# Chunk 7 transposed ahead of the first block's stores, and two products of a seven-product block exchanged

## The chip, the cores and the metric

The kernel runs on one core of one Trainium2 chip. The metric is the device time in microseconds (us) of one execution. Inside the core several engines work side by side, each through its own list of instructions in order: PE (TensorE, matrix products), DVE (VectorE), ACT (ScalarE), POOL (GpSimd) and SP (SyncE, which here issues nearly all DMAs). They wait for each other through semaphores.

## What is computed

The reference, cut to what matters, is a linear attention with a decaying state, followed by a two-layer network with a Mish-like activation:

```python
# q, k, v: (4, 8, 768, 64); w_in: (512, 2048); w_out: (2048, 512)
for t in range(S):
    state = gamma[None, :, None, None] * state + np.einsum('bhd,bhe->bhde', k[:, :, t], v[:, :, t])
    y[:, :, t] = scale * np.einsum('bhd,bhde->bhe', q[:, :, t], state)
...
x = y.transpose(0, 2, 1, 3).reshape(B * S, H * D)          # 3072 tokens x 512
h = x @ w_in
sp = np.where(h > 20.0, h, np.log1p(np.exp(np.minimum(h, 20.0))))
g = h * np.tanh(sp)
out = (g @ w_out).astype(np.float32)
```

## The kernel before

**Tiles and stages.** The 3072 tokens are 24 chunks of 128 (six for each of the 4 batches). The chunks go through the kernel in blocks: block 0 has four chunks (0 to 3), blocks 1 to 10 have two each, so block 1 has chunks 4 and 5, block 2 has 6 and 7, block 3 has 8 and 9, and so on (`first[blk]` is a block's first chunk).

The attention of a chunk g takes these steps. `load` (L135) brings its q, k and v from memory on SP, 256 KB each. `cast_q` (L320, POOL), `cast_k` (L325, ACT) and `cast_v` (L329, POOL) scale them into fp16. `turn_by_dma` (L342) transposes q and k with one DMA on SP; `turn_and_load` (L902) does that and then issues the loads up to chunk g+2. `scores` (L373) multiplies k and q on PE, `mask` (L383) masks them on DVE, `outer` (L390) makes the outer products of k and v on PE, `state_sum` and `state_decay` carry the state on, and `y_two` (L465) makes the attention's output of a whole block from the state (`past`, L416) and the masked scores (`present`, L423). An ACT copy (L475) then leaves it in `xt`, the input of the network.

The network of a block is `g1` (x times w_in, then Mish) and `g2` (times w_out). From block 1 on, half of the first layer is done by `g1_seven` (L597) in a seven-product scheme for 2 x 2 block matrices: sums of weight blocks (`wsums`) and of input blocks (`tsums`, made by `x_sums`, L588) are multiplied, and the results are combined. From block 2 on the second layer uses a seven-product scheme too (`seven`, L689). Block 1 has the plain second layer (L512).

**Order of the work.** The order on each engine is written out by hand: the program's order is each engine's order. Work of the attention for later chunks is put into named places of a block's network by dictionaries, `steps_of` (L927) for blocks from 2 on and `steps_of_half` (L953) for block 1; a function `step(name)` runs what is listed under a name. Numbered places of block 1's second layer are filled by `plan_of` (L963), among them `scores_two` for chunks 6 and 7 at place 10 and `cast_k` of chunk 10 at place 15, the last one.

**Three accumulators.** `g1_seven` uses three accumulators in PSUM, `pb`, `px` and `pe`. The lines between L653 and L668 are what the change touches. The first product goes to px, and ACT copies it out (`snap`, L623) as m1; px is then not cleared, but added to by the second-sum product `mm(px, s(2), t(2))`, and copied again as u2; later the third-sum product `mm(px, s(3), t(3))` is added to it once more. The first-sum product `mm(pe, s(1), t(1))` starts pe afresh, and its copy is m5. A product that adds to an accumulator can start only when the copy taken from it before is finished. At the place "p2", ahead of these, blocks 2 to 9 have `outer_next`, the outer products of the next block's chunks: eight matmuls for two chunks, or four where the second chunk is the last of its batch, whose state is not needed.

**The queue around the stores.** Block 0 leaves four output tiles of 256 KB in a list `stores`, each with the due number 1; `store_due(n)` (L178) issues on SP all that are due by n. In block 1 that happens at the place "p6". The same place scales chunk 7's k and then has chunk 7 transposed, followed by the loads of chunk 9. `op`, the pool of output tiles, has five of these tiles.

Of the kernel before, what the change touches and what calls it, by code (L numbers as in the profile page):

```python
# [16 lines left out]
def kernel(  # L17
# [21 lines left out]
    BLOCKS = [4] + [2] * ((NCK - 4) // 2)  # L39
    first = [sum(BLOCKS[:i]) for i in range(len(BLOCKS))]  # L40
# [56 lines left out]
    for c in range(2):  # L97
        t = tri_first[c * HB:(c + 1) * HB]
# [79 lines left out]
    def store_due(now):  # L178
        while stores and stores[0][0] <= now:
            _, dst, osb = stores.pop(0)  # L180
            nc.sync.dma_start(dst, osb)
# [251 lines left out]
    def last_of_batch(g):  # L433
        return g % NCH == NCH - 1
# [45 lines left out]
    def win(s, f, bp):  # L480
        return wins[s, f // 2][:, bp, f % 2 * P:(f % 2 + 1) * P]
# [13 lines left out]
    def xt(blk, bp):  # L495
        return xts[0][:, :, bp] if blk == 0 else xts[blk][:, bp, :BLOCKS[blk] * C]
# [13 lines left out]
    def g2_mm(o_ps, blk, t, fb, cols=slice(None)):  # L510
        s, f = divmod(fb, FPS)
        nc.tensor.matmul(  # L512
            o_ps, gts[blk, fb][:, t * P:(t + 1) * P], wouts[s][:, f, cols],
            start=(fb == 0), stop=(fb == NFB - 1))

    def g2_out(o_ps, blk, t, due, cols=slice(None), on_act=False):
        osb = op.tile(list(o_ps.shape), FP32, name="osb", tag="osb")
        if on_act:
            nc.scalar.copy(osb, o_ps)
        else:  # L520
            nc.vector.tensor_copy(osb, o_ps)
        row0 = (first[blk] + t) * P
        dst = out[row0:row0 + P, cols]
        stores.append((due, dst, osb))
# [59 lines left out]
    def x_part(blk, i, j):  # L584
        n = NBP // 2
        return xts[blk][:, i * n:(i + 1) * n, j * P:(j + 1) * P]
# [7 lines left out]
        nc.vector.tensor_tensor(t[:, 2], b[1][1], b[0][1], op=sub)  # L594
        nc.vector.tensor_tensor(t[:, 3], b[1][0], t[:, 1], op=sub)

    def g1_seven(blk, steps):  # L597
        n = NBP // 2
        gt = gtiles[blk, 0] = gp.tile([P, NFB, 2 * P], FP16, name="g", tag="g")
        for fb in range(NFB):  # L600
            gts[blk, fb] = gt[:, fb]
        pb, px, pe = [mmps.tile([P, FPS, P], FP32, name="h_ps", tag="mm") for _ in range(3)]

        def a(i, j):
            return lambda f, d: win(2 * i, f, j * n + d)

        def s(i):
            return lambda f, d: wsums[0][:, i - 1, d, f * P:(f + 1) * P]

        def b(i, j):  # L610
            return lambda d: x_part(blk, i, j)[:, d]

        def t(i):
            return lambda d: tsums[blk][:, i - 1, d]

        def mm(h_ps, w, x, first=False):
            for f in range(FPS):
                for d in range(n):
                    nc.tensor.matmul(  # L619
                        h_ps[:, f], w(f, d), x(d), start=first and f == 0 and d == 0,  # L620
                        stop=d == n - 1, skip_group_check=True)

        def snap(h_ps):  # L623
            x = hsnaps[0][:, nsnap[0] % 4].rearrange("p (f t) -> p f t", t=P)
            nsnap[0] += 1
            nc.scalar.copy(x, h_ps)  # L626
            return x

        def mish_of(i, j, h):
            nc.scalar.activation(  # L630
                gt[:, 2 * i * FPS:(2 * i + 1) * FPS, j * P:(j + 1) * P], h, AF.Mish,
                scale=inv_boost3)

        def plus(h_ps, x):
            h = hp.tile([P, FPS, P], FP32, name="hsum", tag="hsum", bufs=3)
            nc.vector.tensor_tensor(h, h_ps, x, op=ALU.add)  # L636
            return h

        def plain(s, half):
            h_ps = mmps.tile([P, 2, 2 * P], FP32, name="h_ps", tag="mm")  # L640
            for j in range(2):
                for bp in range(NBP):
                    nc.tensor.matmul(  # L643
                        h_ps[:, j], win(s, 2 * half + j, bp), xt(blk, bp),
                        start=bp == 0, stop=bp == NBP - 1)
            fb = s * FPS + 2 * half
            nc.scalar.activation(gt[:, fb:fb + 2], h_ps, AF.Mish, scale=inv_boost3)  # L647

        def step(name):
            for fn, *args in steps.get(name, ()):  # L650
                fn(*args)

        mm(px, a(0, 0), b(0, 0), True)  # L653
        m1 = snap(px)
        mm(pb, a(0, 1), b(1, 0), True)
        c11 = plus(pb, m1)
        step("p2")
        mm(pe, s(1), t(1), True)
        m5 = snap(pe)
        mm(px, s(2), t(2))  # L660
        u2 = snap(px)
        mish_of(0, 0, c11)
        step("p6")
        plain(1, 0)
        mm(px, s(3), t(3))
        c22 = plus(px, m5)
        mm(pe, s(4), b(1, 1))
        c12 = plus(pe, u2)  # L668
        mish_of(1, 1, c22)
        mish_of(0, 1, c12)  # L670
        step("p7")
        plain(3, 0)
        mm(px, a(1, 1), t(4))
        mish_of(1, 0, px)
        step("p4")
        plain(1, 1)
        step("h2")
        plain(3, 1)
        step("end")
# [247 lines left out]
    def steps_of(blk):  # L927
        a, nb = first[blk] + 4, blk + 1
        if nb == len(BLOCKS):
            only, then = lambda *work: [], lambda *work: []  # L930
        else:
            only = lambda *work: list(work)
            then = only if a < NCK else lambda *work: []
        return {
            "p2": [*then((gate_x, blk), (cast_q, a)), *only((outer_next, nb), (sum_next, nb, 0),
                   (decay_next, nb, 0)), (cast_v, a)],
            "p6": [(store_due, 1), (turn_and_load, a)],
            "p7": [(store_due, 2), *only((sum_next, nb, 1)), (sums_a, blk, slice(0, FPS))],
            "p4": [(store_due, 3), (sums_a, blk, slice(FPS, FPS + 2))],
            "h2": only((scores, a - 2), (scores, a - 1), (mask, a - 2)),  # L940
            "end": [(sums_a, blk, slice(FPS + 2, 2 * FPS))],
            "m1": [(cast_k, a + 1)],
            "m2": [*only((gate_g, blk), (decay_next, nb, 1)), (cast_q, a + 1), (cast_v, a + 1),
                   *only((mask, a - 1)), (turn_and_load, a + 1)],
            "m7": [*only((y_two, nb)), (cast_k, a + 2)],
            "m3": only((x_sums, nb)),
        }

    def some_late(n):
        for _ in range(min(n, len(late))):  # L950
            late.pop(0)()

    def steps_of_half(blk):  # L953
        a = first[blk] + 4
        return {
            "p2": [(gate_x, blk), (cast_v, a - 1)],
            "p6": [(store_due, 1), (cast_k, a - 1), (turn_and_load, a - 1), (some_late, 1)],
            "p7": [(store_due, 3), (cast_q, a), (some_late, 1)],
            "p4": [(cast_v, a), (some_late, 2)],
            "end": [(cast_k, a), (turn_and_load, a)],  # L960
        }

    def plan_of(blk):  # L963
        a = first[blk] + 4
        return {10: [(scores_two, blk + 1)],
                11: [(cast_q, a + 1), (cast_k, a + 1)],
                12: [(outer_two, blk + 1), (cast_v, a + 1), (turn_and_load, a + 1)],
                14: [(y_two, blk + 1)],
                15: [(cast_k, a + 2)]}
# [5 lines left out]
    for blk in range(1, len(BLOCKS)):  # L975
        if blk >= SEVEN:
            steps = steps_of(blk)
            g1_seven(blk, steps)
            seven(blk, steps, blk + 1 == len(BLOCKS))
            continue  # L980
        g1_seven(blk, steps_of_half(blk))
        n1 = NFB * BLOCKS[blk] // CPB
        plan = plan_of(blk)
        for u in range(n1, 2 * n1):
            store_due(u)
            t, part = divmod(u - n1, 4)
            if part == 0:
                o_ps = mmps.tile([P, d_model], FP32, name="o_ps", tag="mm")
            for fb in range(part * 4, part * 4 + 4):
                g2_mm(o_ps, blk, t, fb)  # L990
            if part == 3:
                g2_out(o_ps, blk, t, u + 3 if t == 0 else 3)
            for fn, *args in plan.get(u, ()):
                fn(*args)
            some_late(1)
        x_sums(blk + 1)
# [31 lines left out]
```

## Time and profile before

| | |
|---|---|
| median of 3 runs | 204.19 us (203.92 to 204.65) |
| the profiled execution's own time | 204.32 us |
| its span, first to last instruction | 202.4 us |
| PE busy | 194.2 us, 96% |
| PE weight loads busy | 152.9 us, 76% |
| DVE busy | 143.5 us, 71% |
| ACT busy | 111.1 us, 55% |
| POOL busy | 67.8 us, 33% |
| bytes moved by DMA | 38.65 MB |
| granted TensorE clock | full speed all along |

All times below are counted from the span's start. A timeline row gives the start, the duration, the engine, the source line, the operation, what it writes from what it reads, and in square brackets the idle time of the engine before it with what ended that. SPq rows are DMA issues: their duration is that of issuing, and the data lands some microseconds later. Ends of matmuls are modelled and overlap the next ones, so the spacing of starts is what a matmul costs. The chain of waits goes back from the last instruction, at each step to what released it.

### The profile page before, as it was taken

What the parts mean: (1) busy time and instruction counts of PE and PEld (TensorE: products, weight loads), DVE (VectorE), ACT (ScalarE), POOL (GpSimd) and SP (SyncE); (2) the same over time, 40 slices, a digit from 0 to 9 for tenths busy, and PEclk for the clock granted to TensorE, in tenths of its full rate; (3) what the DMA queues carried; (4) which work ended last, traced back from release to release, by engine and by line L of the source; (5) the groups of instructions that cost most, each with busy time, mean ns of one, the idle gap of its engine ahead of it and who ended that gap; (6) DMA issues with size and microseconds to landing.
All of it is one profiled execution on the core that took longest, in us unless ns stands there. A gap on an engine that the chain in (4) does not pass through costs nothing.

```text
span 202.4 us, 5431 instructions
## 1 busy us (share of the span) xinstructions
PE 194.2 (96%) x2239; PEld 152.9 (76%) x2239; DVE 143.5 (71%) x271; ACT 111.1 (55%) x199; POOL 67.8 (33%) x83
## 2 busy tenths in 40 slices
PE   6797999999999999999999999999999999999993
PEld 2455544455955788988988988988988988988982
DVE  2677744969879687587696696787696696696552
ACT  2364665242961773774674674674674663753850
POOL 4073000527424337424407607604407616200000
PEclk9999999999999999999999999999999999999999
DMA  4999999998999998996991992999992952200202
GB/s 164 304 312 359 385 386 292 276 263 182 224 272 230 233 221 177 195 224 161 230 206 38 216 243 81 233 183 156 247 205 46 224 98 55 104 3 25 84 26 78
DMA packets 95896, 38.65 MB, mean 191 GB/s; under 512 B 82304, under 2 KB 89984, under 8 KB 95872
## 3 DMA queue, kind: packets, MB, share of 16 engines
q1 hardware_dynamic: 92608, 37.50, 81.2%
q10 hardware_dynamic: 3264, 0.82, 2.2%
q8 instruction: 17, 0.28, 0.6%
q14 instruction: 7, 0.06, 0.1%
HBM read 27.30 MB, written 6.29 MB: 166 GB/s over the span
## 4 chain that ended last, share of the span: by engine, by line
PE 78%; DMA 14%; ACT 2%; DVE 2%; issue 1%; SPq 1%; POOL 1%; POOLq 0%; DVEq 0%
PE o_ps L709 28%; PE h_ps L643 16%; PE h_ps L619 14%; DMA vf<-in_v_dram 6%; PE h_ps L490 6%; DMA qkt<-qk 3%; PE y_ps L429 3%; DMA qfirst<-in_q_dram 2%; DMA kf<-in_k_dram 2%; PE at L379 2%; PE o_ps L512 2%; PE y_ps L419 2%; PE u_ps L393 2%; PE h_ps L782 1%; SPq L132 1%
## 5 line engine op out<-in xcount | busy, mean ns | idle before, releaser
L643 PE MATMUL h_ps<-xt,win 128*128 128x256 f16 x320 | 41.2, 273 | 0.0
L322 POOL TENSOR_TENSOR qk<-qf,qvs 128x512 f16<-128x512 f32 x20 | 23.7, 1186 | 26.4 <-DMA qf<-in_q_dram 25.5
L643 PEld LDWEIGHTS <-win 128*128 128x128 f16 x320 | 29.4, 98 | 3.6
L709 PEld LDWEIGHTS <-gsum 128*128 128x128 f16 x288 | 27.5, 98 | 3.8
L636 DVE TENSOR_TENSOR hsum<-h_ps,hsnap 128x512 f32<-128x512 f32 x30 | 19.8, 688 | 13.9 <-PE h_ps L619 11.5
L647 ACT ACTIVATE g<-h_ps 128x512 f16<-128x512 f32 x40 | 23.7, 593 | 5.6 <-PE h_ps L643 5.5
L385 DVE TENSOR_TENSOR am<-at,tri 128x1024 f16<-128x1024 f32 x20 | 24.2, 1217 | 1.7 <-PE at L379 1.7
L709 PE MATMUL o_ps<-tmat,gsum 128*128 128x256 f16 x216 | 25.1, 273 | 0.0
L626 ACT COPY hsnap<-h_ps 128x512 f32<-128x512 f32 x30 | 16.6, 587 | 13.2 <-PE h_ps L619 13.2
L331 POOL TENSOR_TENSOR v<-vf,qvs 128x512 f16<-128x512 f32 x20 | 21.3, 1064 | 7.4 <-DMA vf<-in_v_dram 7.4
L709 PEld LDWEIGHTS <-g 128*128 128x128 f16 x216 | 21.1, 98 | 2.4
L723 DVE TENSOR_TENSOR osb<-o_ps,snap 128x256 f32<-128x256 f32 x27 | 11.4, 424 | 16.0 <-PE o_ps L709 11.7
L512 PE MATMUL o_ps<-wout,g 128*128 128x512 f16 x96 | 22.7, 379 | 0.0
L630 ACT ACTIVATE g<-hsum 128x512 f16<-128x512 f32 x30 | 18.7, 634 | 4.3 <-DVE hsum L636 4.3
L619 PEld LDWEIGHTS <-wsum 128*128 128x128 f16 x320 | 19.1, 98 | 0.8
L327 ACT ACTIVATE qk<-kf 128x512 f16<-128x512 f32 x20 | 12.6, 632 | 12.1 <-DMA kf<-in_k_dram 7.4
L475 ACT CAST xt<-y_ps 128x1024 f16<-128x1024 f32 x10 | 10.1, 1012 | 16.2 <-PE y_ps L429 16.2
L715 ACT COPY snap<-o_ps 128x256 f32<-128x256 f32 x27 | 10.1, 372 | 15.7 <-PE o_ps L709 15.7
L709 PE MATMUL o_ps<-wout,g 128*128 128x256 f16 x144 | 17.2, 273 | 0.0
L619 PE MATMUL h_ps<-xsum,wsum 128*128 128x128 f16 x240 | 16.6, 219 | 0.0
L340 POOL COPY gate<-gsum 128x1 f16<-128x1 f16 x8 | 1.5, 186 | 44.2 <-DVE gsum L683 44.2
L619 PEld LDWEIGHTS <-win 128*128 128x128 f16 x240 | 15.1, 98 | 1.5 <-issue 0.8
(96 smaller groups left out, 289.9 us busy)
## 6 DMA issues: line engine op xcount, KB each, us to landing
kf<-in_k_dram SPq DMA_DIRECT2D x23, 256.0 KB, 4.5
vf<-in_v_dram SPq DMA_DIRECT2D x23, 256.0 KB, 5.3
out_dram<-osb SPq DMA_DIRECT2D x22, 256.0 KB, 4.3
qf<-in_q_dram SPq DMA_DIRECT2D x19, 256.0 KB, 4.0
wt<-in_moe_w_out_dram SPq DMA_DIRECT2D x3, 1024.0 KB, 8.1
wi<-in_moe_w_in_dram SPq DMA_DIRECT2D x4, 512.0 KB, 7.1
wi<-in_moe_w_in_dram SPq DMA_DIRECT2D x2, 1024.0 KB, 10.7
qfirst<-in_q_dram SPq DMA_DIRECT2D x2, 512.0 KB, 5.5
```

The costliest lines, as they stand in the source:

```text
L322: nc.gpsimd.tensor_tensor(room16(g)[0], loaded[g][0], qs.unsqueeze(2).broadcast_to((P, H, D)), op=ALU.mult)
L327: nc.scalar.mul(room16(g)[1], loaded[g][1], BOOST)
L331: nc.gpsimd.tensor_tensor(room16(g)[2], loaded[g][2], vs.unsqueeze(2).broadcast_to((P, H, D)), op=ALU.mult)
L385: nc.vector.tensor_tensor(am, ats.pop(g), tri.unsqueeze(1).unsqueeze(1).broadcast_to((P, 2, HP, C)), op=ALU.mult)
L512: nc.tensor.matmul(o_ps, gts[blk, fb][:, t * P:(t + 1) * P], wouts[s][:, f, cols], start=(fb == 0), stop=(fb == NFB - 1))
L619: nc.tensor.matmul(h_ps[:, f], w(f, d), x(d), start=first and f == 0 and d == 0, stop=d == n - 1, skip_group_check=True)
L626: nc.scalar.copy(x, h_ps)
L630: nc.scalar.activation(gt[:, 2 * i * FPS:(2 * i + 1) * FPS, j * P:(j + 1) * P], h, AF.Mish, scale=inv_boost3)
L636: nc.vector.tensor_tensor(h, h_ps, x, op=ALU.add)
L643: nc.tensor.matmul(h_ps[:, j], win(s, 2 * half + j, bp), xt(blk, bp), start=bp == 0, stop=bp == NBP - 1)
L647: nc.scalar.activation(gt[:, fb:fb + 2], h_ps, AF.Mish, scale=inv_boost3)
L709: nc.tensor.matmul(o_ps, x(f), w(f), start=first and f == 0, stop=f == n - 1, skip_group_check=True)
```

## The change

There are two edits. In block 1, `cast_k(7)` moves from the place "p6" to a new place "u2", which is right behind the copy of px as u2 and ahead of the first Mish of the block on ACT. At "p6", `turn_and_load(7)` comes first and the stores follow; the due number there rises from 1 to 3, and the separate `store_due(3)` at "p7" goes. On SP this puts one transposition and the three loads of chunk 9 ahead of the four stores. On ACT it exchanges two neighbours, the scaling and the Mish.

In `g1_seven`, a flag `sum_first` puts the second-sum product and its copy ahead of the first-sum product and its copy. The flag is set where the next block exists and its second chunk is not the last of a batch, that is in blocks 2, 4, 5, 7 and 8. These are the blocks with two chunks' outer products at "p2". No instruction is added or removed on any engine.

```diff
-    def g1_seven(blk, steps):
+    def g1_seven(blk, steps, sum_first=False):
...
         step("p2")
+        if sum_first:
+            mm(px, s(2), t(2))
+            u2 = snap(px)
         mm(pe, s(1), t(1), True)
         m5 = snap(pe)
-        mm(px, s(2), t(2))
-        u2 = snap(px)
+        if not sum_first:
+            mm(px, s(2), t(2))
+            u2 = snap(px)
+        step("u2")
         mish_of(0, 0, c11)
         step("p6")
...
             "p2": [(gate_x, blk), (cast_v, a - 1)],
-            "p6": [(store_due, 1), (cast_k, a - 1), (turn_and_load, a - 1), (some_late, 1)],
-            "p7": [(store_due, 3), (cast_q, a), (some_late, 1)],
+            "u2": [(cast_k, a - 1)],
+            "p6": [(turn_and_load, a - 1), (store_due, 3), (some_late, 1)],
+            "p7": [(cast_q, a), (some_late, 1)],
...
-            g1_seven(blk, steps)
+            g1_seven(blk, steps, blk + 1 < len(BLOCKS) and not last_of_batch(first[blk + 1] + 1))
```

In block 1, `a` is 8, so `a - 1` is chunk 7.

## The prediction

> **What bounds the kernel now.** I read the busy table first (PE, TensorE, is busy 96% of the 202.4 us span), then the chain of waits, which from 61 us to the end is a string of PE pieces. A change can therefore pay only where PE itself stands, and I looked for those places. In the chain and the waits there is one near the edit:
>
> ```profile
> 51.61 3.74 DMA vf<-in_v_dram
> 55.35 5.61 DMA qkt<-qk
> 60.96 0.05 issue
> 61.01 0.40 PE at L379 x8
> ```
> ```profile
> PE at L379 <- DMA qkt<-qk: 0.4, 1, 0.4
> ```
>
> The transposition of chunk 7, issued at 55.35, lands 5.61 us later, and the scores of chunk 7 (L379) wait for it. The timeline (start, duration, engine, line) shows what stood ahead of it on the DMA queue SP, the scaling of its k behind a Mish on ACT (ScalarE), and what undisturbed scores cost:
>
> ```profile
> 52.59 2.60 SPq L181 DMA_DIRECT2D out_dram<-osb  x4
> 55.35 2.46 SPq L344 DMA_TRANSPOSE qkt<-qk  x1
> ```
> ```profile
> 53.36 0.64 ACT L630 ACTIVATE g<-hsum 128x512 f16<-128x512 f32 x1
> 53.89 0.63 ACT L327 ACTIVATE qk<-kf 128x512 f16<-128x512 f32 x1
> ```
> ```profile
> 60.16 0.40 PE L379 MATMUL at<-qkt 64*128 64x128 f16 x8
> 61.01 0.40 PE L379 MATMUL at<-qkt 64*128 64x128 f16 x8 [0.45 <-DMA qkt<-qk]
> 61.34 1.90 PE L512 MATMUL o_ps<-wout,g 128*128 128x512 f16 x8
> ...
> 73.65 0.62 PE L379 MATMUL at<-qkt 64*128 64x128 f16 x16
> 74.20 1.05 PE L643 MATMUL h_ps<-xt,win 128*128 128x256 f16 x8
> ```
>
> Sixteen score products take 74.20-73.65 = 0.55 us in block 2, but 61.34-60.16 = 1.18 here: the stall costs 0.63 us. Six microseconds later, at the start of block 2, comes the piece that decides my forecast:
>
> ```profile
> 67.89 0.63 ACT L327 ACTIVATE qk<-kf 128x512 f16<-128x512 f32 x1 [0.63 <-DMA kf<-in_k_dram]
> 68.42 0.57 ACT L626 COPY hsnap<-h_ps 128x512 f32<-128x512 f32 x1
> ```
> ```profile
> 68.20 0.61 PE L393 MATMUL u_ps<-v,qk 128*128 128x128 f16 x8
> 68.64 1.06 PE L619 MATMUL h_ps<-xsum,wsum 128*128 128x128 f16 x16
> 69.54 1.04 PE L643 MATMUL h_ps<-xt,win 128*128 128x256 f16 x8
> ```
>
> ACT works in the order of the program. Its copy m1 (L626) stands behind the scaling of chunk 10's k (L327), and that waits for the load, which lands at 67.86 (issued 63.68, 4.2 us to landing). So m1 ends at 68.99, 1.13 us behind the landing. PE does not notice today: after the outer products (L393) it runs the first-sum product into pe for 0.45 us (half of 69.54-68.64) and needs m1 only for the second-sum one into px, at 69.09.
>
> **The change part by part.**
>
> (1) *The scores' stall.* cast_k(7) takes the place of the Mish at 53.36 and ends at 53.99 instead of 54.52. SP is free at 52.49 (its last load issue), stands until then, and issues the transposition at about 54.05. With the transposition of chunk 6, issued on an almost equally filled queue, issue to landing took 4.1 us, so chunk 7's lands at 58.2. The scores need it at 60.16 plus half of 0.55, 60.4: 2.2 us of cover. The 0.63 us goes. Behind it nothing takes it back: VectorE's two masks end at 62.95 in both kernels, the copy L521 (62.88 to 63.57) and the state L402 (0.69) behind them end by 64.3, and PE's past product (L419), now at 65.25, would come at 64.62. So block 2 begins 0.63 earlier, at 66.68.
>
> (2) *The Mish moved back* by 0.53 us ends at 54.5; its first reader, the second layer of block 1 (L512), starts at 57.48: 3 us of cover. The work behind it on ACT keeps its place, since both instructions stay ahead of it. It costs nothing; without cover it would cost 0.53.
>
> (3) *The DMA queue.* The transposition and three loads (q, k, v of chunk 9) pass four stores of 256 KB on SP; the next transposition and chunk 10's loads follow the stores. No bytes change, so the landing L of chunk 10's k moves only by idle time made or saved. Spacing of landings now, from issue starts and times to landing: v(8) 56.1; stores to 59.8 (3.7); transposition 61.0 (1.1); q, k, v of chunk 9 62.2, 63.4, 64.5 (1.2 each, 1.1 the last); transposition of 8 65.3 (0.8); q(10) 66.65 (1.35); k(10) 67.86 (1.2). In the stores' 3.7 lies a hole:
>
> ```profile
> 56.00:58.40 2.40, 2.40 (x21) 1.77 (x19) 2.37 (x4) 2.37 (x6) 1.33 (x1) 1.00 1.07 376
> 58.40:59.60 1.20, 1.20 (x7) 0.53 (x6) 0.98 (x2) 0.39 (x1) 0.00 (x0) 1.00 1.31 52
> ```
> ```profile
> q8 instruction: 1, 0.02, 4.8%
> ```
>
> (columns: window, its length, busy time of PE, PEld, DVE, ACT and POOL, clock, DMA share, GB/s). For 1.2 us the engines hold packets but move 52 GB/s instead of 376. The last line is the DMA view of 55.9 to 57.2: one instruction packet of 16 KB held one of the 16 engines for 1 us (4.8% of 16 times 1.3). That engine's share of the stores runs late, and the transposition begins on all engines only when it is through. So the stores really need 2.5 us.
>
> After: transposition issue 54.05 to 55.9 (1.85, as chunk 6's), q(9) issued then and landing 3.5 us later, as the load behind chunk 6's transposition did (50.36 to 53.89): 59.4. Then k 1.2, v 1.1, stores 2.5, transposition 1.0 (after a store elsewhere 0.9 to 1.0), q 1.35, k 1.2: L = 59.4+8.35 = 67.8. Bounds: with the shortest issue (1.24) and q's shortest latency (3.4) q(9) lands at 58.7 and L is 67.05; with the longest issue (2.46) and 4.0 us for q, as behind the transposition of 143.7, q(9) comes at 60.5 and L at 68.8; a transposition kept by the held engine lies inside that. I take 67.8, the row of chunk 6.
>
> The Trainium skill says otherwise of the hole: "DMA: Bandwidth & Descriptors", section "Two DMAs through the same engine are not ordered", states that "Nothing at all orders DMAs across the 16 engines". The window at 58.4 does not agree for a transposition; what that rule gives is a rival below.
>
> (4) *The second-sum product first* (blocks 2, 4, 5, 7, 8). In every block PE stands 0.06 us before the third-sum product: in block 2 it starts at 70.47, eight products of 0.109 behind 69.54 would allow 70.41, and the copy u2 ends at 70.42. With px first, u2 ends half a microsecond sooner: 0.06 saved per block. The price is that PE needs m1 right behind the outer products. In blocks 4, 5, 7 and 8 it is there: block 8's m1 ends at 157.16+0.58 = 157.74, PE comes at 157.85. These four give -0.24.
>
> In block 2 it is not there. Px cannot start before X = L+1.18 (m1, then 0.05 to PE, as between 70.42 and 70.47), nor before 68.01 (68.64 less 0.63). Behind X come two half products (0.89) and the plain one (0.87), so the third-sum product starts at X+1.77 = L+2.95, against 70.47. Block 2 thus shifts the rest by L-67.52, whatever (1) saved; only for L under 66.83 does all of it survive (-0.69 with the 0.06).
>
> **Sum.** Net = L-67.52-0.24 = L-67.76. With L = 67.8 that is +0.04: the 0.63 us taken from the scores is given back as PE waiting about 1 us for m1 in block 2. On the profiled execution's own 204.32 us (span 202.4 and 1.9 around it) this makes 204.36; the median shown, 204.19, is 0.13 lower, so 204.2 on its scale; I say 204.3. A difference under 0.3% (0.61 us) is about what cannot be told from none.
>
> **Rivals.**
> - *All gains survive* (faster). L comes so early that m1 is ready, or nearly: from L under 67.15 net is beyond -0.61, to -0.93 at 66.83: 203.3 to 203.6. For: the 1.2 us hole might be passed while the queue is empty anyway. Against: even the shortest rows give 67.05. Chance 0.18.
> - *Chunk 10's key late* (slower): one mechanism, the empty DMA time around 56 plus the held engine under the transposition of 7, push L past 68.37; at 68.8 net is +1.04, 205.2. For: SP stands 1.5 us with nothing to issue, and the page shows the DMA engines 90% busy in that stretch. Against: SP reaches chunk 10's loads at about the same time as before. Chance 0.28.
> - *No waiting for the held engine*: the transposition lands near 57.3 and q(9) by its own latency at 58.9, L 67.3: net -0.46, 203.7. The window at 58.4 speaks against it. Chance 0.06. This is what the sentence of the Trainium skill quoted above would make of it.
> - *The transposition is no earlier where it counts*: it would have to land after 60.4, 6.3 us from its issue; the longest of 18 took 5.6. The time stays 204.2. Chance 0.02.
>
> **How the numbers follow.** Forecast 0.46. Faster 0.18; slower 0.28; within 0.3% 0.46+0.06+0.02 = 0.54. The range takes L from 67.05 to 68.8: -0.71 and +1.04 on 204.19, 203.5 to 205.2. The likeliest case alone holds 203.6 to 204.8.
>
> **What would show it.** The L379 wait on the transposition is gone and the transposition lands near 58.2; block 2's first product starts near 66.7; PE shows a wait on ACT's L626 of 0.8 to 1.2 us in block 2, with ACT L327 there waiting over 1.5 us for chunk 10's k; blocks 4, 5, 7 and 8 are 0.06 us shorter and 3, 6, 9 unchanged. I am wrong if chunk 10's k lands well off 67.8, or if px in block 2 starts without waiting.

## The result and the profile after

The changed kernel took 205.59 us (median of 9 executions, 204.34 to 206.06), the kernel before, on the same chip, 204.44 us (9 executions, 203.92 to 204.86). The ratio is 1.0049, with a 95% interval of 1.0026 to 1.0071: slower by half a per cent. The forecast was no change, 204.3 us.

The profile that came with the result is of the quickest of the nine executions, 204.34 us with a span of 202.5 us. It shows the steps of the prediction almost number by number, and that makes it misleading. First PE in the timeline:

```profile
59.98 0.62 PE L379 MATMUL at<-qkt 64*128 64x128 f16 x16
60.53 1.90 PE L512 MATMUL o_ps<-wout,g 128*128 128x512 f16 x8
...
66.50 1.05 PE L619 MATMUL h_ps<-xt,win 128*128 128x128 f16 x16
67.39 0.61 PE L393 MATMUL u_ps<-v,qk 128*128 128x128 f16 x8
69.02 1.05 PE L619 MATMUL h_ps<-xsum,wsum 128*128 128x128 f16 x16 [1.02 <-ACT hsnap L626]
69.91 1.04 PE L643 MATMUL h_ps<-xt,win 128*128 128x256 f16 x8
70.79 0.61 PE L619 MATMUL h_ps<-xsum,wsum 128*128 128x128 f16 x8
```

The sixteen score products now run in one piece (60.53-59.98 = 0.55 us), and the wait on the transposition is gone. In block 2 PE stands 1.02 us for m1, the ACT copy L626. Before the third-sum product (70.79) the 0.06 us are gone: 69.91 and eight products of 0.109 make 70.78. The same stretch on ACT:

```profile
65.44 1.01 ACT L475 CAST xt<-y_ps 128x1024 f16<-128x1024 f32 x1 [3.89 <-PE y_ps L429]
67.87 0.63 ACT L327 ACTIVATE qk<-kf 128x512 f16<-128x512 f32 x1 [1.42 <-DMA kf<-in_k_dram]
68.41 0.57 ACT L626 COPY hsnap<-h_ps 128x512 f32<-128x512 f32 x1
```

The scaling of chunk 10's k waits for its load until 67.85, and m1 stands behind it. This execution lost the 0.63 us in block 2 that it had gained in block 1, as forecast, and its span is 0.1 us longer than the first one's. But it is an execution of 204.34 us, and the median is 1.25 us above it. No profile shows one of the longer executions on this chip; what they do is read below from profiles taken on other chips. One execution of `a_after_again`, 208.35 us at a granted clock of 0.992 where the others show 0.998 to 1.000, is left out of the times below.

### The profile page after: what moved, and what is told of

Read it like the earlier page. It is cut to its first block, busy times and chain, and to the rows that moved or that the text cites. A ratio compares the mean times of both kernels' runs of the same rounds, so it can differ in the third digit from the quotient of the medians.

```text
span 202.5 us, 5430 instructions
## 1 busy us (share of the span) xinstructions
PE 194.2 (96%) x2239; PEld 153.3 (76%) x2239; DVE 142.5 (70%) x271; ACT 111.2 (55%) x199; POOL 68.6 (34%) x83
## 4 chain that ended last, share of the span: by engine, by line
PE 84%; DVE 5%; DMA 5%; ACT 3%; SPq 2%; issue 1%; DVEq 0%
PE o_ps L714 28%; PE h_ps L643 16%; PE h_ps L619 15%; PE o_ps L512 7%; PE h_ps L490 6%; PE y_ps L429 3%; PE at L379 3%; DMA qfirst<-in_q_dram 2%; DMA kf<-in_k_dram 2%; PE y_ps L419 2%; PE u_ps L393 1%; DVE tmat L545 1%; PE h_ps L787 1%; SPq L344 1%; SPq L181 1%
## 5 line engine op out<-in xcount | busy, mean ns | idle before, releaser
L643 PEld LDWEIGHTS <-win 128*128 128x128 f16 x320 | 29.4, 98 | 3.6
L322 POOL TENSOR_TENSOR qk<-qf,qvs 128x512 f16<-128x512 f32 x20 | 24.3, 1214 | 22.5 <-DMA qf<-in_q_dram 22.5
L626 ACT COPY hsnap<-h_ps 128x512 f32<-128x512 f32 x30 | 16.6, 587 | 13.6 <-PE h_ps L619 13.6
L410 POOL TENSOR_TENSOR st<-su,gcm 128x512 f16<-128x512 f32 x11 | 14.0, 1271 | 7.4 <-DVE su L405 7.4
```

Of the source, the lines that this page charges most:

```text
L322: nc.gpsimd.tensor_tensor(room16(g)[0], loaded[g][0], qs.unsqueeze(2).broadcast_to((P, H, D)), op=ALU.mult)
L410: by.tensor_tensor(states[g], sus.pop(g), gcm, op=ALU.mult)
L643: nc.tensor.matmul(h_ps[:, j], win(s, 2 * half + j, bp), xt(blk, bp), start=bp == 0, stop=bp == NBP - 1)
```

## The experiments

Each kernel ran beside the kernel before on the same chip, in three groups on three chips. The medians of before were 204.06 us for the first four kernels below (203.93 to 204.13), 204.09 for the next four (`before_again` to `i_products_k10_behind`, 203.92 to 204.22) and 204.34 for the last four, where they spread from 203.69 to 205.69. Ratios are to before of the same group; they are taken over the executions, not from the two medians. L is again the landing of chunk 10's k in a kernel's profile.

**The changed kernel once more** (`a_after_again`, no edit).

> The changed kernel unaltered. Theory M (the wait on m1 in block 2 sets the time, and the landing L of chunk 10's k differs between executions): the median is again 205.4 to 205.8, and an execution that takes 205.5 has L near 69.0 and a wait of PE on ACT L626 of about 2.2 us, against 67.85 and 1.02 us in the profile at hand. Rival E (the extra microsecond lies elsewhere, in blocks where m1 is ready only 0.05 us early, or ahead of block 1): L stays within 0.3 us of 67.9 and the time shows up in another stretch.

205.11 us, ratio 1.0055 (1.0043 to 1.0068); the profiled execution is the one of 205.11. Its PE timeline:

```profile
60.76 0.62 PE L379 MATMUL at<-qkt 64*128 64x128 f16 x16
61.31 1.90 PE L512 MATMUL o_ps<-wout,g 128*128 128x512 f16 x8
...
68.17 0.61 PE L393 MATMUL u_ps<-v,qk 128*128 128x128 f16 x8
69.84 1.05 PE L619 MATMUL h_ps<-xsum,wsum 128*128 128x128 f16 x16 [1.05 <-ACT hsnap L626]
70.73 1.04 PE L643 MATMUL h_ps<-xt,win 128*128 128x256 f16 x8
71.60 0.61 PE L619 MATMUL h_ps<-xsum,wsum 128*128 128x128 f16 x8
```

The wait on m1 is as long as before, 1.05 us, not 2.2. But everything stands 0.8 us later: block 2's third-sum product starts at 71.60 instead of 70.79, since L is 68.66 instead of 67.85, and the scores of chunk 6 already start at 60.76 instead of 59.98. Both theories are half wrong: L is later, though not at 69.0, and time was lost ahead of block 1 as well. The waits of PE in this execution say where:

```profile
PE at L379 <- DVE qkt L370: 1.2, 1, 1.2
PE h_ps L619 <- ACT hsnap L626: 1.1, 1, 1.1
```

PE stood 1.2 us until 42.55, at the scores of chunk 4, for a copy of DVE (L370). Neither the first profile of before nor that of after has this wait. It became theory U below.

**The queue alone** (`b_queue_only`).

```diff
-            g1_seven(blk, steps, blk + 1 < len(BLOCKS) and not last_of_batch(first[blk + 1] + 1))
+            g1_seven(blk, steps)
```

> Only the queue order and the earlier scaling of chunk 7; the products in their old order in all blocks. Theory M: block 2 needs m1 0.45 us later, the other four blocks lose their 0.06 each, so 0.45-0.24 = 0.2 us less than the changed kernel: 205.3 to 205.4, still slower than before by 0.8 to 1.0. Rival E with the products at fault: the time returns to 203.6 to 204.0, the 0.63 us of the scores gained.

204.96 us, ratio 1.0043 (1.0030 to 1.0056). The queue order with the earlier scaling makes the kernel slower; the products are not at fault. It is 0.15 us below the changed kernel by the medians and 0.28 by the means, where 0.2 was expected. In its profile L is 68.43, and PE waits 0.59 us for m1, behind the first-sum product.

**The products alone** (`c_products_only`): the queue and the scaling of chunk 7 as before.

> Only the exchanged products, the queue as before. Theory M: L stays at 67.86, block 2 shifts by 67.86-67.52 = +0.34, the four other blocks give -0.24: +0.1, 204.4 to 204.7. Rival E with the products at fault: slower by about 1 us, 205.4.

203.78 us, ratio 0.9990 (0.9981 to 0.9998): 0.28 us less than before by the medians and 0.21 by the means, near five times 0.06. L is 67.29, so m1 was not late here, and block 2 gave its 0.06 too. The price that I had put on the exchange in block 2 (+0.34) needs an L of 67.86, the first profile's.

**The old order in block 2 alone** (`d_block2_old`).

```diff
-            g1_seven(blk, steps, blk + 1 < len(BLOCKS) and not last_of_batch(first[blk + 1] + 1))
+            g1_seven(blk, steps, blk > SEVEN and blk + 1 < len(BLOCKS) and not last_of_batch(first[blk + 1] + 1))
```

> The changed kernel with the old order of products in block 2 alone. Theory M: 0.45 us less than the changed kernel, about 205.1, as the wait on m1 moves behind the first-sum product but stays. If m1's wait were worth only what the profile at hand shows (1.02 us), the time would be 204.0.

204.55 us, ratio 1.0031 (1.0019 to 1.0042): 0.56 us less than the changed kernel by the medians and 0.50 by the means, where 0.45 was expected. It is not quite an even comparison: this kernel's profile has an L of 68.37, against 68.66. The wait on m1 stays (0.52 us, behind the first-sum product) and the kernel is slower than before.

**The kernel before, a second profile** (`before_again`).

> The kernel before, for a second profile. Theory U (in most executions the scores of chunk 7 don't wait at all before the change, since PE already lost 0.6 us or more at the scores of chunk 4): PE waits 1.1 to 1.5 us there on DVE L370, the scores of chunk 6 start near 60.8, the transposition of chunk 7 has landed by then (near 60.4), and chunk 10's k lands near 67.3, so m1 is not waited for. Rival P (the first profile is the usual case): a wait of about 0.6 us at chunk 7's scores, none at chunk 4's.

204.04 us. The waits of PE and its timeline:

```profile
PE at L379 <- DVE qkt L370: 1.5, 1, 1.5
```
```profile
60.60 0.62 PE L379 MATMUL at<-qkt 64*128 64x128 f16 x16
61.16 1.90 PE L512 MATMUL o_ps<-wout,g 128*128 128x512 f16 x8
...
68.02 0.61 PE L393 MATMUL u_ps<-v,qk 128*128 128x128 f16 x8
68.46 1.06 PE L619 MATMUL h_ps<-xsum,wsum 128*128 128x128 f16 x16
69.36 1.04 PE L643 MATMUL h_ps<-xt,win 128*128 128x256 f16 x8
70.29 0.61 PE L619 MATMUL h_ps<-xsum,wsum 128*128 128x128 f16 x8
```

Theory U holds: the scores run in 0.56 us with no wait. The stall of 0.63 us that the prediction was built on is not there; PE has lost its time at chunk 4, and chunk 7's transposition, behind the stores, lands at 60.09 and is needed at about 60.9. Of the eleven profiles of kernels that leave DVE's order alone, eight show this wait at chunk 4, 1.1 to 1.5 us; the two first ones and one more (`j_scaling_only`) do not. The eight are all the profiles of the first two groups; on the chip of the result both profiles are without it, so that the longer executions there show the same wait is inferred, not seen. The wait is not all loss either: in the eight, PE transposes chunk 4 (L366) at 39.4 to 39.9 and starts its scores at 42.3 to 42.6, in the other three at 40.2 to 40.5 and at 41.7 to 42.0. They come 0.3 to 1.2 us earlier and leave 0.4 to 0.9 us later. Chunk 10's k lands at 67.17 here.

**Where L goes.** The DMA queue in `before_again`, then in `a_after_again`:

```profile
50.86 1.04 SPq L132 DMA_DIRECT2D vf<-in_v_dram  x1
51.99 2.47 SPq L181 DMA_DIRECT2D out_dram<-osb  x4
55.03 1.41 SPq L344 DMA_TRANSPOSE qkt<-qk  x1
```
```profile
50.75 0.87 SPq L132 DMA_DIRECT2D vf<-in_v_dram  x1
54.66 2.16 SPq L344 DMA_TRANSPOSE qkt<-qk  x1
56.87 0.58 SPq L132 DMA_DIRECT2D qf<-in_q_dram  x1
```

Before, SP issues the stores from 51.99 on. After, it has nothing to issue from 51.62 to 54.66, 3.0 us, because the transposition waits for ACT's scaling, and that comes with PE's block 1. What that does to the DMA engines is seen in the windows, again `before_again` and then `a_after_again` (the last two columns are the DMA share and GB/s):

```profile
55.40:57.00 1.60, 1.60 (x21) 1.49 (x19) 1.60 (x2) 1.60 (x4) 1.04 (x1) 1.00 1.06 405
```
```profile
55.40:57.00 1.60, 1.60 (x21) 1.47 (x20) 1.60 (x4) 1.60 (x4) 1.04 (x1) 1.00 0.86 82
```

82 GB/s for 1.6 us, where the stores moved 405 before and loads move about 220 (51.6 to 54.6 in `a_after_again`). The engines first work off the loads already issued (209 GB/s from 54.0 to 54.5); from 54.5 to 59.0 they move 87 GB/s, against 275 in `before_again`. The same bytes stand ahead of chunk 10's k in both kernels, but after the change DMA time went by nearly unused, and k lands later: L is 68.15 to 68.66 in the four profiles with the changed queue in these groups, and 67.17 to 67.59 in the three with the old one.

**Chunk 10's scaling behind u2** (`e_k10_behind`): the changed kernel, with ACT's order altered in block 2.

```diff
-                14: [(y_two, blk + 1)],
-                15: [(cast_k, a + 2)]}
+                14: [(y_two, blk + 1)]}
...
             steps = steps_of(blk)
+            if blk == SEVEN:
+                steps["u2"] = [(cast_k, first[blk] + 4)]
```

> The changed kernel with the scaling of chunk 10's k moved on ACT from ahead of m1 to behind u2 in block 2. Theory M (all of the loss comes through that scaling ahead of m1): chunk 10's k still lands near 68.4 to 68.7, but PE waits for nothing in block 2; the time falls below before by the five blocks' 0.06, 203.6 to 203.9. Rival D (the later DMA queue costs elsewhere as well): it stays above 204.3.

203.76 us, ratio 0.9985 (0.9976 to 0.9994). L is 68.15, late as in the changed kernel, and PE's timeline has no wait left in block 2:

```profile
67.97 0.61 PE L393 MATMUL u_ps<-v,qk 128*128 128x128 f16 x8
68.42 1.06 PE L619 MATMUL h_ps<-xsum,wsum 128*128 128x128 f16 x16
69.31 1.04 PE L643 MATMUL h_ps<-xt,win 128*128 128x256 f16 x8
70.19 0.61 PE L619 MATMUL h_ps<-xsum,wsum 128*128 128x128 f16 x8
```

One instruction moved on ACT turns +0.5% into -0.15%. The later DMA queue costs nothing else that these times can tell.

**Two of the stores first** (`h_two_stores_first`): the due numbers of the four stores become `t // 2`, and `(store_due, 0)` heads the place "p2" of block 1.

> The changed kernel with two of the four stores issued ahead of chunk 7's transposition, while SP has nothing else to do, and two behind chunk 9's loads. Theory H (the loss is empty time of the DMA engines while SP waits for chunk 7's scaling): the two stores fill it, chunk 10's k lands near 67.3 to 67.6 instead of 68.4 to 68.7, the wait on m1 is under 0.2 us, the time is 203.7 to 204.1. Rival O (the order itself, stores ahead of chunk 10's loads, makes them late): the same bytes stand ahead of chunk 10's k, it lands near 68.5 and the time stays near 205.

203.91 us, ratio 0.9998 (0.9989 to 1.0007). The loss is gone, though no gain is left over. In the profiled execution, which took 204.33 us and is one of the longer ones, L is 67.79, outside the 67.3 to 67.6 expected, and PE still waits 0.26 us for m1:

```profile
PE h_ps L619 <- ACT hsnap L626: 0.3, 1, 0.3
```

Rival O, by which the time stays near 205, is out. Filling the empty time is what brings L back: two stores take up part of it, and L comes 0.4 us sooner than in `e_k10_behind` on the same chip and 0.9 sooner than in `a_after_again`. The time is filled only in part: L is still 0.2 to 0.6 us later than with all stores first.

**The products with chunk 10's scaling behind u2** (`i_products_k10_behind`): `c_products_only` and the edit of `e_k10_behind`.

> The queue as before, the products exchanged, and the scaling of chunk 10's k behind u2 in block 2. Theory M: with chunk 10's k landing near 67.3 nothing was waited for in c_products_only, so moving it changes nothing: 203.7 to 203.9. If the scaling ahead of m1 cost something in c_products_only too, the time is lower by up to 0.3.

203.76 us, ratio 0.9985 (0.9977 to 0.9994), the same as `c_products_only` and as `e_k10_behind`. Where L is early, the place of the scaling does not matter; and with m1 freed, the new queue order is worth nothing here against the old one.

**The earlier scaling of chunk 7 alone** (`j_scaling_only`).

```diff
-            "p6": [(store_due, 1), (cast_k, a - 1), (turn_and_load, a - 1), (some_late, 1)],
+            "u2": [(cast_k, a - 1)],
+            "p6": [(store_due, 1), (turn_and_load, a - 1), (some_late, 1)],
```

> The kernel before with chunk 7's scaling ahead of the first Mish of block 1 and nothing else. Theory M: SP is behind the four stores when the scaling ends either way, so the transposition is not earlier and the time is that of before within 0.15%. If the exchange on ACT itself cost (the later Mish), the time would rise by up to 0.5 us.

204.22 us, ratio 0.9991 (0.9974 to 1.0008): no difference. Its profile is the third one without the wait at chunk 4. The sixteen score products of chunks 6 and 7 take 0.81 us there (59.86 to 60.67), so they lose 0.26 and not 0.63, and this execution took 203.72 us.

**One sum of DVE out of the way.** Three kernels tried whether the two waits are tied. `weight_sums` leaves DVE sums that are dropped in between; the first (L542) stands ahead of chunk 4's L370. The edit puts it behind that chunk's scores, and moves the second one (L543) from ahead of chunk 5's L370 to behind it.

```diff
-            if u in (NFB + 5, NFB + 8):
+            if u in (NFB + 8, NFB + 10):
```

In the kernel before (`l_before_sum_later`):

> The kernel before with the same sum moved. Theory U: the 0.6 us gained at chunk 4's scores bring PE to chunk 7's scores before the transposition behind the stores has landed (about 60.1), so a wait of 0.3 to 0.5 us appears there, as in the first profile, and only 0.1 to 0.3 us are gained: 203.8 to 204.0. If the two waits are not tied in this way, the whole 0.6 is gained: 203.4.

204.12 us, ratio 0.9993 (0.9976 to 1.0010): not told from no gain. PE's waits in its profile:

```profile
PE at L379 <- DMA qkt<-qk: 0.5, 1, 0.5
PE at L379 <- DVE qkt L370: 0.2, 1, 0.2
```

The wait at chunk 4 has shrunk to 0.2 us, and the wait for chunk 7's transposition is back, 0.5 us long, as in the first profile. The whole 0.6 us is not gained (the interval ends at 0.49), which fits theory U: what is gained at one wait goes into the other. The two do not always come to the same sum: the profile of `j_scaling_only` has neither in full.

In the changed kernel (`m_after_sum_later`):

> The changed kernel with the same sum moved. Chunk 7's scaling, and with it its transposition and chunk 10's k, come up to 0.6 us earlier too; the wait on m1 stays near 1 us: 204.5 to 204.9, still slower than before.

204.88 us, ratio 1.0021 (1.0003 to 1.0038), still slower. L is 68.55, and the wait on m1 is 1.6 us in its profile, not 1: what PE gained at chunk 4 it waits for there. L was expected up to 0.6 us earlier. The transposition is issued that much earlier than in `a_after_again` (54.04 against 54.66), but L is only 0.1 us earlier. So the time of that issue does not settle L alone; what else did is open.

In `e_k10_behind` (`k_e_and_sum_later`):

> e_k10_behind with one sum of weight blocks (L542, 0.68 us on DVE) moved from ahead of chunk 4's copy L370 to behind the scores that wait for it. Theory U (what hides the stall of chunk 7 is PE's earlier wait on L370): that wait falls from 1.4 to about 0.8 us, block 1 and all behind it start 0.6 us earlier, chunk 7's transposition still lands ahead of its scores, 203.0 to 203.3. If another wait ends at the same place, nothing or little is gained: 203.6 to 203.8.

203.54 us, ratio 0.9952 (0.9936 to 0.9969): 0.80 us below the kernel before and faster than both kernels, if not quite down to the 203.3 expected. With neither the transposition nor m1 in the way, PE keeps the time. It is 0.58 us below `l_before_sum_later`, and five times 0.06 is 0.3 of that. The rest may be a first sign that the earlier transposition pays; no run separates it from the place of chunk 10's scaling, and the executions of `l_before_sum_later` spread over 0.86 us.

## Why the prediction was wrong

Two terms of the sum L-67.52-0.24 failed, both because they were read from one execution: the landing L of step (3), and the base 67.52, which holds the stall of step (1).

*The scores' stall, step (1).* "The 0.63 us goes" was right for the profiled execution and wrong for most: of the four further profiles with the old queue and DVE's order, three show no stall at chunk 7 (`before_again`, `c_products_only`, `i_products_k10_behind`) and one 0.26 us (`j_scaling_only`). I took the stall as belonging to the kernel; it is there only when PE comes early to block 1. In `before_again` PE has waited 1.5 us at chunk 4 and finds the transposition landed. There is nothing to gain at the scores then, and the third-sum product of before starts at 70.29, not 70.47: the base is 0.18 us lower, and the net higher by that.

*The DMA queue, step (3)*: this is the larger error. The mechanism was right, and in the profile that came with the result the size too (L forecast at 67.8, measured 67.85), but partly by luck: the transposition's issue took 1.24 us instead of 1.85, and q of chunk 9 took 4.5 us to land instead of 3.5. In `a_after_again` L is 68.66, 0.86 more than forecast. What failed is the first term: q(9) lands at 60.39 instead of 59.4 (59.80 in `b_queue_only`), while the terms behind it, forecast at 8.35, measured 8.27 (8.63 there). I let SP stand 1.5 us; it stands 3.0, since its loads are issued 0.9 us earlier (v of chunk 8 at 50.75 instead of 51.61) while ACT's scaling comes 0.6 us later than forecast (53.95 instead of 53.36), behind a PE that has waited. So 0.86 and 0.18 make the forecast of +0.04 into +1.08.

*The products, step (4)*: right. The third-sum product at L+2.95 gives 70.80 and 71.61; measured 70.79 and 71.60. The 0.06 per block came in `c_products_only`. Put together for two profiles with the wait at chunk 4: 71.60 in `a_after_again` against 70.29 in `before_again` is +1.31, and four times 0.06 less is +1.07. These two executions took 205.11 and 204.04 us, on two chips; on the chip of `a_after_again` the medians of after and before differ by 1.05, and in the result by 1.15.

*The Mish moved back, step (2)*: right, no cost (`j_scaling_only`).

*The rivals.* The slower one, chunk 10's key late, is what happened, by the empty DMA time that it named; its deciding point, 68.37, is passed in `a_after_again`. The time still came out above its 205.2 and the range, for two reasons: in `before_again` the third-sum product is at 70.29, not 70.47, so that the same L costs 0.18 more, and the median of before is 204.44 over the nine executions of the result, against 204.19 over the first three of them, which the range was built on. The rival without waiting for the held DMA engine got no support: in the first profile after, the transposition landed at 58.05, q of chunk 9 at 59.61 and L was 67.85; forecast 58.2, 59.4 and 67.8, and by the rival 57.3, 58.9 and 67.3.

Not tried: why chunk 5's q lands earlier in some executions than in others. The profiles show only what that does to DVE and to PE (last section).

## What to carry to other kernels

A stall seen in one profile may be the place where a loss shows itself in that execution, not the loss: look for a second profile, or for another engine that was late further up, before counting on it. When a queue entry that waits for another engine is moved ahead of entries that are ready, count how long the queue then stands with nothing to issue, and follow that time to the next load that somebody waits for. And an instruction that waits for a load should not stand on its engine ahead of a short copy that the busiest engine needs: in the changed kernel, whose L is late, moving that one instruction took the loss away; with the old queue, whose L is early, it was worth nothing (`i_products_k10_behind`).

## What the runs showed of the hardware

The copy L370 is late at chunk 4 because a sum on DVE ahead of it takes three times as long while POOL works. The row of DVE before a collision, the POOL instruction, and the row in it, all from the timeline of `before_again`:

```profile
39.19 0.43 DVE L581 TENSOR_TENSOR wsum<-wsum,win 128x512 f16<-128x512 f16 x1
...
39.40 1.11 POOL L322 TENSOR_TENSOR qk<-qf,qvs 128x512 f16<-128x512 f32 x1 [1.20 <-DMA qf<-in_q_dram]
39.53 1.27 DVE L581 TENSOR_TENSOR wsum<-win,win 128x512 f16<-128x512 f16 x1
```

The same sum took 0.42 us in the first profile, where the load of chunk 5's q came later and POOL's instruction started at 40.30. It is so in all eleven profiles: where POOL starts at 39.3 to 39.6 the sum takes 1.26 or 1.27 us and PE waits at chunk 4 (eight), and where it starts at 40.3 to 40.6 the sum takes 0.42 and PE does not wait (three). The Trainium skill, "SBUF — State Buffer", section "Who interferes with whom", says that a two-input DVE instruction with both inputs in SBUF contends with GpSimd's reads; 0.42 against 1.27 us agrees with it. So 0.85 us on DVE hang on when a load lands, and with them PE's arrival at block 1. No run moves POOL's instruction to test it.
